# Sixteen single moves in a hand-written order of steps: polysketch attention and a multiplicative FFN on one core

## The chip, the core and the metric

The kernel runs on one core of a Trainium2 chip. The metric is the device time of one execution in microseconds (us), as the median of several runs.

## What is computed

Two blocks in a row, all in float32. The first is linear attention over 4 batches of 4 heads with 1088 tokens of 32 numbers; its feature map `phi` is the outer product of two sketches with 8 numbers each. The second is an FFN on 4352 tokens with 128 numbers, whose hidden layer (1024 wide) is the product of two projections.

```python
def phi(x):
    a = np.einsum('rd,bhsd->bhsr', S1, x)
    b = np.einsum('rd,bhsd->bhsr', S2, x)
    return np.einsum('bhsi,bhsj->bhsij', a, b).reshape(*x.shape[:-1], r * r)
q_p, k_p = (phi(q), phi(k))
kv = np.einsum('bhsf,bhsd->bhfd', k_p, v)
z = np.sum(k_p, axis=2)
num = np.einsum('bhsf,bhfd->bhsd', q_p, kv)
den = np.einsum('bhsf,bhf->bhs', q_p, z)[..., None] + 1e-06
x = (num / den)            # bridge: (B,H,S,D) -> (B*S, H*D)
h = (x @ w1) * (x @ w2) @ w3
out = h @ w_out
```

## The kernel before

**How the work is cut.** `make_steps` (L150) defines 1179 named steps, each with one or a few instructions, and the kernel issues them in the order of the hand-written list `ORDER` (L75). Each engine (PE the matrix unit, DVE the vector engine, ACT the scalar engine, POOL GpSimd, SP the engine that issues DMAs) executes its own instructions in that order, chained one behind the other; between engines only true dependences on data and buffers wait. So a move in `ORDER` changes the work of those engines alone that find other steps of theirs between the old place and the new.

**Which engine a step takes** is set by four sets of names: what calls `on(name)` goes to DVE, or to POOL where the name is in `POOL` (L53), or to ACT (`ACTS`); a copy by `cp(name)` goes to ACT, or to DVE where the name is in `CPV` (L65).

**Which buffer it takes** is dealt by `SLOTS` (L28): for each kind of tile a string with one digit per tile in the order in which the tiles are made. "b" deals the eight PSUM banks, "m" 32 SBUF buffers of 2 KB a row, "l" 13 larger ones. A tile waits for the last reader of the tile that had its buffer before.

**The stages**, by the names of their steps:

- `k0` to `k3` are the four batches of k. `k3.gram0` to `k3.gram4` (L659) build a Gram matrix with 144 small matmuls 32x64 and 32x32, `Gm`, `Gt`, `Ga`, `Gb`, `Gc` split it (on DVE, `Gc` on ACT), and `T0`, `T1`, `N0`, `N1` are small products behind it. `k2.rest0`, which the Gram of k2 needs, and `k2.kT1`, `k3.rest0` prepare k on POOL and ACT.
- `q0` to `q3` are groups of 512 tokens of q, `q4` and `q6` groups of 1024, `qr` the last 256. A group goes through `max`, `l1`, `l2`, `rm` (peak and scales), `sl`, `sca`, `sh` (splits), `al`, `bs` (the two sketches), `p01`, `p2`, `p12`, `dn`, `de`, `rc` (denominator), `phi0` (L1509, outer product), `pT0` (L1517, a transposition on DVE), `x` (L1527, 64 products 32x32 into four banks) and `xT0` to `xT3` (L1540, copies out of the banks: four on DVE or ACT for each step of a wide group). `q4.ns` (L1494) is a row of short POOL operations for scales.
- `w0` to `w10` turn the weights from 64-bit words into float32: `load`, `c` (ACT), `m`, `j` (DVE, some `m` on ACT), `a0`, `a1` (POOL). At most four large loads are under way (`UNDER_WAY`, L1880). `f0` to `f7` fold `w3` and `w_out` into `w3o`. `s.RC` (three copies on POOL) and `s.AR` spread the sketch matrices.
- FFN groups `g0` to `g3` have 512 tokens each. For each of eight column blocks c: `g{n}.{c}a` (L1799, product with w1), `g{n}.{c}c` (L1804, copy to SBUF), `g{n}.{c}b` (L1809, product with w2), `g{n}.{c}m` (L1815, their product on DVE, called ab). `g{n}.{c}o` (L1835) multiplies ab with `w3o` and sums up in one bank of the group, `g{n}.oT` (L1842) transposes that bank on DVE, and the store follows. The last 256 tokens are the group `gr`.
- FFN groups 4 to 7 go two by two by a scheme with seven products for eight (`seven`, L1633; names `h4`, `h6`). For each of four blocks i and each of the two weights (`a`, `b`): products `h4.2a1` to `h4.2a7` (L1673; an `a` and a `b` product use half of PE's rows each), copies and sums `c` to `i` (L1680 and others), multiplications `m11`, `m12`, `m22` (L1707), `m21`, sums `T1` to `T4` (L1727 to L1742), and products `P1` to `P7` (L1759; 64 columns each, low or high half).

**Around the change.** Ahead of `q3.x` DVE takes the multiplications of groups 1 and 2, `k3.Gm` to `k3.Gb`, `k3.kT0` and the copy `g2.3c`; `q3.x` takes four banks, the last of which DVE's multiplications give back. Ahead of `qr.x` the products `g1.7o`, `g0.1o`, `g0.0o`, `g0.5o`, `g0.7o`, `g1.0o`, `g3.5o` stand on PE, then `q6.x`; on DVE `g0.oT` and then `qr`'s chain from `p01` to `phi0`, with `p01`, `p2`, `p12`, `bs` on POOL, and behind it the eight copies of `q6.xT0` and `q6.xT2` and `qr.pT0`; `q6.xT1` and `q6.xT3` are ACT's. `h4.s2` and the `T` sums of `POOL` are POOL's.

Of the kernel before, what the change touches and what calls it, by code (L numbers as in the profile page):

```python
# [86 lines left out]
q1.Ct g0.4c g0.4b q1.sh q1.sl k1.rest0 g0.7b w0.c1 g0.7a k1.abt w0.j1 k1.gram0 w0.c0 q1.scy k1.gram1 kh2.load q1.sca  # L87
q2.tr g0.5c q1.al q1.p01 q1.p2 k1.gram2 k1.gram3 kr1.abc k1.gram4 w6.load w0.m0 g0.6b w0.j0 g0.7c g0.7m k1.Gm q1.p12
k1.Gc g0.0a w2.load w0.a1 q1.dn q1.de q1.rc q1.bs k1.Gt g0.3a k1.Ga k2.kT1 k1.Gb g0.3c q1.restT g0.2a q1.phi k1.T0
k1.T1 q1.pt0 g0.4m w0.a0 q2.max q2.l2 g0.6a k1.Ta k2.lead0 k2.rest0 g0.1a g0.2c k1.Tc g0.5b q3.tr g0.5m k1.Tb q1.pc0  # L90
q1.pt1 g0.1b w9.load s.RC k1.N0 s.AR q2.l1 q2.rm v3.zero q1.pc1 k1.N1 q1.x g0.6c g0.1c k1.Na k1.Nr k3.zero k2.gram0
# [1843 lines left out]
```

## Time and profile before

| | us |
|---|---|
| median of 3 runs | 246.07 |
| lowest and highest run | 245.98, 246.84 |
| the profiled execution's own time | 246.81 |
| its span, from first to last instruction | 245.0 |
| PE busy, share of the span | 237.3, 97% |
| DVE busy | 208.7, 85% |
| POOL busy | 162.5, 66% |
| ACT busy | 123.6, 50% |

The profile lists busy time by engine, the chain of work that ended last (followed back from the last instruction), and for PE what each idle stretch waited for (a row "PE tile line <- releaser tile line: total, count, longest"). A row of the grouped instructions in a window reads: start in us, busy time, engine, line, operation, out<-in, size, count; a bracket at its end is the idle time of the engine just before and what ended it. A row of the table by stretches reads: window, its length, then busy time and count of PE, PE's weight loads, DVE, ACT and POOL, then the granted PE clock, the DMA share and GB/s. A row of the chain reads: start, length, engine, tile, line. A float32 product of 512 columns leaves two records on PE, so `x10` there are five products.

### The profile page before, as it was taken

The page shows a single profiled execution, that of the slowest core. Times are in us where ns is not written, and L with a number is a line of the kernel's source. Part 1 is how long each engine was busy: PE and PEld are TensorE (multiplying, and loading weights), DVE is VectorE, ACT ScalarE, POOL GpSimd, SP SyncE. Part 2 cuts the span into 40 slices and gives each one's busy share as a digit, 9 for nine tenths or more (in the row PEclk, how much of TensorE's full clock was granted, in tenths as well). Part 3 has the DMA queues.
Part 4 walks back from the last instruction along what each step waited for, and adds up shares of the span by engine and source line. Part 5 has one row for each costly group of instructions (what it writes and reads, how often), then busy time and mean ns, then how long its engine had stood idle before and what let it go on. Part 6 is the DMA issues. An engine that isn't in the chain of part 4 may idle for free.

```text
span 245.0 us, 6748 instructions
## 1 busy us (share of the span) xinstructions
PE 237.3 (97%) x2724; PEld 132.8 (54%) x2724; DVE 208.7 (85%) x421; ACT 123.6 (50%) x245; POOL 162.5 (66%) x204
## 2 busy tenths in 40 slices
...
GB/s 209 258 112 321 147 226 218 46 208 209 238 117 262 191 207 206 37 1 3 3 0 3 1 0 3 59 112 3 1 0 0 0 3 0 0 1 3 11 92 91
DMA packets 31935, 22.06 MB, mean 90 GB/s; under 512 B 21280, under 2 KB 26528, under 8 KB 31904
## 3 DMA queue, kind: packets, MB, share of 16 engines
...
q14 instruction: 10, 0.08, 0.1%
...
## 4 chain that ended last, share of the span: by engine, by line
PE 84%; DVE 8%; ACT 3%; issue 2%; POOL 1%; ACTq 0%; POOLq 0%; DVEq 0%
PE ps_X L1673 11%; PE a_ps L1799 10%; PE ps_o L1759 10%; PE b_ps L1809 10%; PE ps_o L1835 9%; PE ps_Y L1673 6%; PE ps_w3o L534 5%; PE idle_ps L255 4%; PE ps_Z L1673 3%; PE ps_ac L1374 2%; PE ps_x L1527 2%; PE ps_g L659 2%; PE ps_kv L769 2%; PE ps_or L1824 2%; DVE ab L1815 2%
## 5 line engine op out<-in xcount | busy, mean ns | idle before, releaser
L1673 PE MATMUL ps_X<-xd,wv 64*128 64x512 f32 x112 | 36.3, 593 | 0.0
L1799 PE MATMUL a_ps<-xT,w 128*128 128x512 f32 (+1 forms) x80 | 35.9, 560 | 0.0
L1809 PE MATMUL b_ps<-xT,w 128*128 128x512 f32 (+1 forms) x80 | 35.6, 555 | 0.0
L1804 ACT COPY ffa<-a_ps 128x512 f32<-128x512 f32 (+1 forms) x37 | 19.8, 541 | 28.7 <-PE a_ps L1799 25.6
L1707 POOL TENSOR_TENSOR hc<-hc 128x512 f32<-128x512 f32 x16 | 20.6, 1302 | 13.8 <-DVE hc L1685 13.5
L1835 PE MATMUL ps_o<-ab,w3o 128*128 128x512 f32 x64 | 29.6, 600 | 0.0
L1680 ACT COPY hc<-ps_X 128x512 f32<-128x512 f32 x38 | 21.1, 591 | 16.4 <-PE ps_X L1673 13.5
L1815 DVE TENSOR_TENSOR ab<-ffa,b_ps 128x512 f32<-128x512 f32 (+1 forms) x40 | 24.0, 624 | 5.1 <-PE b_ps L1809 4.2
L501 POOL TENSOR_TENSOR w3c<-w3c,cv_m 128x512 int32<-128x512 int32 x16 | 21.2, 1344 | 4.4 <-DVE w3c L495 4.4
L1799 PEld LDWEIGHTS a_ps<-xT,w 128*128 128x128 f32 x80 | 14.1, 189 | 14.4 <-issue 8.6
L1673 PEld LDWEIGHTS ps_X<-xd,wv 64*128 64x128 f32 x112 | 15.4, 186 | 12.0 <-issue 9.2
L1809 PEld LDWEIGHTS b_ps<-xT,w 128*128 128x128 f32 x80 | 14.4, 190 | 13.1 <-issue 8.3
L1673 PE MATMUL ps_Y<-xd,wv 64*128 64x512 f32 x48 | 19.6, 594 | 0.0
L1835 PEld LDWEIGHTS ps_o<-ab,w3o 128*128 128x128 f32 x64 | 11.6, 190 | 13.4 <-issue 13.0
L534 PEld LDWEIGHTS ps_w3o<-wo,w3T 128*128 128x128 f32 x128 | 15.3, 192 | 2.4 <-issue 2.4
L534 PE MATMUL ps_w3o<-wo,w3T 128*128 128x128 f32 x128 | 15.7, 276 | 0.0
L1759 PE MATMUL ps_o<-hc,w3o 128*64 128x512 f32 x32 | 15.1, 595 | 0.0
L1759 PE MATMUL ps_o<-tt,ws 128*64 128x512 f32 x32 | 13.7, 595 | 0.0
L263 ACT ACTIVATE cv_c<-raw 128x1024 f32<-128x1024 f32 (+1 forms) x13 | 13.0, 1017 | 0.0
L1680 ACT COPY hc<-ps_Y 128x512 f32<-128x512 f32 x14 | 8.1, 593 | 9.7 <-PE ps_Y L1673 7.0
L1540 ACT COPY xd<-ps_x 64x256 f32<-64x256 f32 x24 | 8.8, 367 | 7.2 <-PE ps_o L1835 6.8
L538 ACT COPY w3o<-ps_w3o 128x128 f32<-128x128 f32 x8 | 2.1, 272 | 19.7 <-PE ps_w3o L534 19.7
...
## 6 DMA issues: line engine op xcount, KB each, us to landing
...
```

What stands on the lines that cost most here:

```text
L263: act.activation(dst, hi.bitcast(F32), ACT.Prelu, scale=2.0 ** -112, alpha=-2.0 ** 32)
L501: pool.tensor_tensor(d, d, x["m"][:, i * 512:(i + 1) * 512], ALU.add)
L534: pe.matmul(t["o"], w3T[ko][:, c], wo[:, c], start=c == 0, stop=c == NC - 1)
L1673: pe.matmul(x[bank], stat(j, u)[:, i * 128:(i + 1) * 128], rows(j, u), start=new, stop=True, tile_position=(u * 64, 0), skip_group_check=True)
L1680: cp(n(y))(x[k], x[bank])
L1707: on(f"h{g}.{i}m{k}").tensor_mul(both[0][k], both[0][k], both[1][k])
L1759: pe.matmul(acc_o[bank][half[0]:half[1]], w(i), x(i), start=n == 1, stop=n == (2 if j == 3 else 4), tile_position=(0, half[0]), skip_group ...
L1799: pe.matmul(x["a"][:, :w], w_of(0, c), xT[g][:, c0:c0 + w], start=True, stop=True)
L1804: cp(f"g{g}.{c}{su}c")(x["s"][:, :w], x["a"][:, :w])
L1809: pe.matmul(x["b"][:, :w], w_of(1, c), xT[g][:, c0:c0 + w], start=True, stop=True)
L1815: dve.tensor_mul(ab_sb[g, c][:, c0:c0 + w], x["s"][:, :w], x["b"][:, :w])
L1835: pe.matmul(o_ps[g], w3o[:, c], ab_sb[g, c], start=n == 1, stop=n == NC)
```

## The change

The first 182 steps of `ORDER` stay as they are; SP's order stays as a whole. Behind them steps move, two change engine, and `SLOTS` follows (three strings, a few digits each):

- `s.RC` goes from behind `w9.load` up to behind `w0.c0`: on POOL ahead of `q1.sca`.
- `k1.T0` goes ahead of `k2.kT1`: on PE ahead of `g0.2a`.
- `g2.6c` and `k3.rest0` go behind `g2.4b`: on ACT `w5.m` now stands ahead of `g2.6c`.
- `q2.restT`, `w6.m`, `w5.j`, `w2.j` go ahead of `q4.l2`: on ACT `w6.m` now stands ahead of it.
- `g2.1a` goes from behind `w5.m` to behind `k3.Gc`: on PE behind the Gram of k3 and `g2.2a`.
- `g2.3c` goes from DVE to ACT.
- `g2.5m` goes ahead of `g2.7c` and `g2.7m`; `qr.l1`, `qr.rm` ahead of `q4.sl`; `qr.sl` ahead of `q6.dn`.
- `g1.7o` goes from behind `q6.phi1` to behind `g0.oT`: on PE behind `g3.5o`, still ahead of `q6.x`.
- `qr.pT0` goes right behind `qr.phi0`: on DVE ahead of the eight copies.
- `h4.2ac`, `h4.2a6` go ahead of `h4.1ah`: on PE `h4.2a6` ahead of `h4.2a2`, `h4.2b6`.
- `h4.2T2` goes from POOL to DVE.
- `h6.1P4`, `h6.0P1`, `h6.3m21` go ahead of `h6.3m22`.

With the banks dealt anew, `q3.x` waits for `g2.3m` and no longer for `g2.1m`, `qr.x` waits for the copies of `q6.xT2` too, `g1.0b` now waits for `g2.6c`, and `q4.l1` no longer waits for `f2.t`.

```diff
 POOL = set("""
-    g4.oS g5.oS g6.oS g7.oS h4.0T1 h4.0T2 h4.0T3 h4.0m12 h4.0m22 h4.1T2 h4.1m11 h4.1m12 h4.2T2
-    h4.2m11 h4.2m12 h4.2m22 h4.3m11 h4.s2 h4.s4 h6.0T2 h6.0m11 h6.0m12 h6.0m22 h6.1T2 h6.1T3 h6.1m11
+    g4.oS g5.oS g6.oS g7.oS h4.0T1 h4.0T2 h4.0T3 h4.0m12 h4.0m22 h4.1T2 h4.1m11 h4.1m12 h4.2m11
+    h4.2m12 h4.2m22 h4.3m11 h4.s2 h4.s4 h6.0T2 h6.0m11 h6.0m12 h6.0m22 h6.1T2 h6.1T3 h6.1m11 h6.1m12
...
 CPV = set("""
-    g0.0c g0.1c g2.3c h4.1ac h4.1ad h6.1bc h6.2ad k0.kT1 k1.kvc k2.kT1 k2.kq k3.kT0 k3.kT1 k3.kq
-    q0.xc0 q0.xc1 q6.xT0 q6.xT2
+    g0.0c g0.1c h4.1ac h4.1ad h6.1bc h6.2ad k0.kT1 k1.kvc k2.kT1 k2.kq k3.kT0 k3.kT1 k3.kq q0.xc0
+    q0.xc1 q6.xT0 q6.xT2
...
-k2.Na g1.3m g2.6c k3.rest0 g2.4a g2.3a w5.m g2.1a g2.4b g1.0b k2.Nr q3.rc g1.1m g1.4m g1.6b k2.Nb g0.2b kr1.kp w6.j
-q4.tr g2.4c g1.6m w7.load w7.c q3.bs q4.max q4.l2 w3.load w9.a0 k3.gram0 q2.restT w6.m w5.j w2.j k3.gram1 k3.gram2
-q3.load w7.j q3.phi0 k3.gram3 k3.gram4 g2.2a k3.Gc g1.0m w2.a0 g2.6b g2.0a g2.4m g2.1c f6.t w6.a0 w4.load g2.3b w2.a1
+k2.Na g1.3m g2.4a g2.3a w5.m g2.4b g2.6c k3.rest0 g1.0b k2.Nr q3.rc g1.1m g1.4m g1.6b k2.Nb g0.2b kr1.kp w6.j q4.tr
+g2.4c g1.6m w7.load w7.c q3.bs q4.max q2.restT w6.m w5.j w2.j q4.l2 w3.load w9.a0 k3.gram0 k3.gram1 k3.gram2 q3.load
+w7.j q3.phi0 k3.gram3 k3.gram4 g2.2a k3.Gc g2.1a g1.0m w2.a0 g2.6b g2.0a g2.4m g2.1c f6.t w6.a0 w4.load g2.3b w2.a1
...
-g1.5o q4.xT0 qr.sl qr.sc qr.al q6.rc q6.bs q4.xT1 q6.nb q6.na q6.nm q6.nr q6.ne v.1 q6.nn q6.phi0 q4.xT3 q6.phi1 g1.7o
-o.S3 q6.pT0 h4.s1 q6.pT1 g0.1o g0.0o g0.5o g0.7o g1.0o h4.s2 g3.5o g0.oT q6.x g1.1o g2.5o qr.p01 qr.p2 qr.p12 qr.dn
-g3.3o qr.de qr.rc qr.bs qr.phi0 g3.2o q6.xT0 q6.xT1 q6.xT2 o.S1 g2.2o v.2 g3.7o q6.xT3 qr.pT0 qr.x qr.xT0 g1.3o g2.0o
+de g1.5o q4.xT0 qr.sc qr.al q6.rc q6.bs q4.xT1 q6.nb q6.na q6.nm q6.nr q6.ne v.1 q6.nn q6.phi0 q4.xT3 q6.phi1 o.S3
+q6.pT0 h4.s1 q6.pT1 g0.1o g0.0o g0.5o g0.7o g1.0o h4.s2 g3.5o g0.oT g1.7o q6.x g1.1o g2.5o qr.p01 qr.p2 qr.p12 qr.dn
+g3.3o qr.de qr.rc qr.bs qr.phi0 qr.pT0 g3.2o q6.xT0 q6.xT1 q6.xT2 o.S1 g2.2o v.2 g3.7o q6.xT3 qr.x qr.xT0 g1.3o g2.0o
```

**First place: DVE ahead of `q3.x`.** The rows are the end of DVE's work ahead of that step: `G_t` is `k3.Gt`, `kT` is `k3.kT0`, the copy `ffa` is `g2.3c`, `G_a` and `G_b` are `k3.Ga` and `k3.Gb`.

```order
 L201 SCALAR_TENSOR_TENSOR G_t<-G_g,ps_g 128x32
 L720 STREAM_TRANSPOSE kT<-kh 128x512
-L1804 COPY ffa<-a_ps 128x512
 L204 SCALAR_TENSOR_TENSOR G_a<-G_g,G_t 128x32
 L865 TENSOR_TENSOR G_b<-ps_g,G_a 128x32
```

The copy has left DVE; ACT takes it among its copies of group 2. On PE the place where `g2.1a` arrives is the end of the Gram of k3; `ps_g` is the Gram's bank, `w_81` the converted weights.

```order
 L659 MATMUL ps_g<-kk 32x64
 L659 MATMUL ps_g<-k,kk 32x32
-L1799 MATMUL a_ps<-xT,w_81 128x512
+L1799 MATMUL a_ps<-xT,w_81 128x512 x2
 L1809 MATMUL b_ps<-xT,w_81 128x512
 L1799 MATMUL a_ps<-xT,w_81 128x512
```

Two a products follow the Gram now, `g2.2a` and `g2.1a`, in place of one.

**Second place: PE ahead of `q6.x`.** The rows are the eight o products there before the change; `ps_o_2228` is the bank of group 1, `ps_o_2214` that of group 0, and `ab_1251` is the ab of `g1.7o`.

```order
L1835 MATMUL ps_o_2228<-ab_1349,w3o_83 128x512
L1835 MATMUL ps_o_2228<-ab_1251,w3o_83 128x512
L1835 MATMUL ps_o_2214<-ab_976,w3o_83 128x512
L1835 MATMUL ps_o_2214<-ab_1309,w3o_83 128x512
L1835 MATMUL ps_o_2214<-ab_900,w3o_83 128x512
L1835 MATMUL ps_o_2214<-ab_824,w3o_83 128x512
L1835 MATMUL ps_o_2228<-ab_1597,w3o_83 128x512
L1835 MATMUL ps_o_2137<-ab_2254,w3o_83 128x512
```

After the change the same eight stand so (two ab tiles carry other numbers since copies are made in another order):

```order
L1835 MATMUL ps_o_2228<-ab_1349,w3o_83 128x512
L1835 MATMUL ps_o_2214<-ab_976,w3o_83 128x512
L1835 MATMUL ps_o_2214<-ab_1309,w3o_83 128x512
L1835 MATMUL ps_o_2214<-ab_903,w3o_83 128x512
L1835 MATMUL ps_o_2214<-ab_827,w3o_83 128x512
L1835 MATMUL ps_o_2228<-ab_1597,w3o_83 128x512
L1835 MATMUL ps_o_2137<-ab_2254,w3o_83 128x512
L1835 MATMUL ps_o_2228<-ab_1251,w3o_83 128x512
```

`g1.7o` has gone from the second place to the last, and the four products that fill group 0's bank stand one place earlier. `g0.oT` waits for the last of them.

**Third place: DVE behind `qr.phi0`.** `s_rc` is `qr.rc`, `ph` is `qr.phi0`, `pT` is `qr.pT0`, the eight `xd` are `q6.xT0` and `q6.xT2`.

```order
 L1454 RECIPROCAL s_rc<-s_rc 128x8
 L1509 TENSOR_TENSOR ph<-s_al,s_bs 128x512
+L1517 STREAM_TRANSPOSE pT<-ph 128x512
 L1540 COPY xd<-ps_x 64x256 x8
-L1517 STREAM_TRANSPOSE pT<-ph 128x512
 L1842 STREAM_TRANSPOSE oT<-ps_o 128x512 x3
 L1654 TENSOR_TENSOR xd<-xd 128x512
```

The transposition that `qr.x` needs now stands ahead of the eight copies and no longer behind them.

More of the change, by code (lines that the diff above doesn't have):

```diff
@@ L29 @@
     "b":
-        "012345670214657210671306537457462512346127340273014526045421752342140327540542370673245716"
-        "210605643174306534710724534104562761504514502371054643535436051532410354273245554744570504"
+        "012345670214657210671306537457462512346127340273014526045721472352140327540542370673245716"
+        "210605643174306437107523543106572361507514502371054643535436051532410354273245554744570504"
         "7734023146507073701426351241254057163771361764573436046273673572571236574127105",
@@ L34 @@
     "l":
-        "0123456789a7486797c0864b7705995a34b20138c73b92bc0b4879c146a281ba56271a564b60303643a19ca32c"
+        "0123456789a7486797c0864b7705995a34210b38c73b92bc0b4879c146a281ba56271a564b60303643a19ca32c"
         "c2076b",
     "m":
-        "0123456789aejo96p3ke3rfjo7p5t8g50lfin6q8o4donmgp19fh2og3hi5601au6v4jm8emhubcusv6vjgo2olsjs"
+        "0123456789aejo96p3ke3rfjo7p5t8g50lfin6q8o4donmgp19fh2og3hi5601au6v4jm8emhubcusv62jgo6olsjs"
         "aolp8s0h8roj26gk1ivl8hb3mcu0a5pn7tfd9qe0umb4p5j1e2tkmgjeno5rcub7tjkume92fka4ud5tkbigpq10lv"
@@ L53 @@
 POOL = set("""
-    g4.oS g5.oS g6.oS g7.oS h4.0T1 h4.0T2 h4.0T3 h4.0m12 h4.0m22 h4.1T2 h4.1m11 h4.1m12 h4.2T2
-    h4.2m11 h4.2m12 h4.2m22 h4.3m11 h4.s2 h4.s4 h6.0T2 h6.0m11 h6.0m12 h6.0m22 h6.1T2 h6.1T3 h6.1m11
-    h6.1m12 h6.1m22 h6.2T1 h6.2T4 h6.2m11 h6.3T3 h6.3m11 h6.s1 h6.s2 h6.s4 k0.Nf k0.Nh k0.Nr k0.kp1
-    k1.Nr k1.kp1 k2.kp0 k2.kp1 k2.rest0 k3.kp0 k3.kp1 q0.al q0.p01 q0.phi1 q0.sca q1.al q1.bs q1.p12
+    g4.oS g5.oS g6.oS g7.oS h4.0T1 h4.0T2 h4.0T3 h4.0m12 h4.0m22 h4.1T2 h4.1m11 h4.1m12 h4.2m11
+    h4.2m12 h4.2m22 h4.3m11 h4.s2 h4.s4 h6.0T2 h6.0m11 h6.0m12 h6.0m22 h6.1T2 h6.1T3 h6.1m11 h6.1m12
+    h6.1m22 h6.2T1 h6.2T4 h6.2m11 h6.3T3 h6.3m11 h6.s1 h6.s2 h6.s4 k0.Nf k0.Nh k0.Nr k0.kp1 k1.Nr
+    k1.kp1 k2.kp0 k2.kp1 k2.rest0 k3.kp0 k3.kp1 q0.al q0.p01 q0.phi1 q0.sca q1.al q1.bs q1.p12
     q1.phi q1.sca q2.bs q2.p2 q2.phi0 q2.sc q2.sl q3.al q3.bs q3.p01 q3.p12 q3.p2 q3.phi0 q3.sc
@@ L86 @@
 w0.load k1.lead0 q0.xc0 q0.xc1 k0.kq w1.a1 k2.max q0.xt1 k1.ab q0.xT0 q0.xT1 g0.4a q1.load g0.5a q1.sm w0.m1 q1.st
[L87 to L91, printed above, removed]
+q1.Ct g0.4c g0.4b q1.sh q1.sl k1.rest0 g0.7b w0.c1 g0.7a k1.abt w0.j1 k1.gram0 w0.c0 s.RC q1.scy k1.gram1 kh2.load
+q1.sca q2.tr g0.5c q1.al q1.p01 q1.p2 k1.gram2 k1.gram3 kr1.abc k1.gram4 w6.load w0.m0 g0.6b w0.j0 g0.7c g0.7m k1.Gm
+q1.p12 k1.Gc g0.0a w2.load w0.a1 q1.dn q1.de q1.rc q1.bs k1.Gt g0.3a k1.Ga k1.T0 k2.kT1 k1.Gb g0.3c q1.restT g0.2a
+q1.phi k1.T1 q1.pt0 g0.4m w0.a0 q2.max q2.l2 g0.6a k1.Ta k2.lead0 k2.rest0 g0.1a g0.2c k1.Tc g0.5b q3.tr g0.5m k1.Tb
+q1.pc0 q1.pt1 g0.1b w9.load k1.N0 s.AR q2.l1 q2.rm v3.zero q1.pc1 k1.N1 q1.x g0.6c g0.1c k1.Na k1.Nr k3.zero k2.gram0
 g0.1m k2.gram1 k2.gram2 q3.max k2.gram3 g0.0c k2.kT0 k1.Nb q1.xT k2.gram4 q3.l2 k2.ab q2.A0 q2.C0 q2.C1 q3.l1 k1.kp0
@@ L107 @@
 q4.st k2.kv0 w4.a1 k3.kp0 k2.kv3 k2.kv1 k2.kv2 k2.kvr q4.sh qr.l2 k3.kv0 k3.kv1 f3.t k2.kvc k3.kv3 k3.kv2 k3.Na w4.a0
-q4.sl q4.sc qr.l1 qr.rm q4.al k3.kvr k3.kvc g3.4a q6.l2 g3.4c g3.4b q4.p01 k3.Nr g3.3b q6.l1 w8.c g3.5a k3.Nb g2.4o
+qr.l1 qr.rm q4.sl q4.sc q4.al k3.kvr k3.kvc g3.4a q6.l2 g3.4c g3.4b q4.p01 k3.Nr g3.3b q6.l1 w8.c g3.5a k3.Nb g2.4o
 g3.4m f1.t f3.m w10.c k3.kqt g3.5c w8.m g3.3m q4.p2 q6.rm k3.kq f1.m f1.o q6.A0 q6.C0 w10.j q6.C1 g3.1o f3.o w8.j
```

11 lines of the change are left out of this document (6 added, 5 removed).

## The prediction, made before the changed kernel ran

> **What bounds the kernel now.** I read the page first, then who waited for whom on PE, then the busy time by stretch.
>
> ```profile
> PE 237.3 (97%) x2724; PEld 132.8 (54%) x2724; DVE 208.7 (85%) x421; ACT 123.6 (50%) x245; POOL 162.5 (66%) x204
> ...
> PE 84%; DVE 8%; ACT 3%; issue 2%; POOL 1%; ACTq 0%; POOLq 0%; DVEq 0%
> ...
> PE ps_g L659 <- issue: 1.6, 2, 1.1
> ...
> PE ps_ph L1246 <- POOL ph L1208: 0.6, 1, 0.6
> PE ps_x L1527 <- DVE pT L1517: 0.4, 1, 0.4
> ...
> 74.00:85.00 11.00, 10.89 (x213) 6.62 (x212) 10.65 (x20) 7.43 (x9) 8.58 (x7) 1.00 0.91 226
> 85.00:152.00 67.00, 67.00 (x795) 38.85 (x786) 60.19 (x117) 31.23 (x65) 48.64 (x41) 1.00 0.19 45
> ```
>
> The reader is to see an engine without room: PE is busy 97% of the span and is 84% of the chain that ended last; from 85 to 152 us it is busy 67.00 of 67.00. The work on PE is the same before and after, so the change can gain only what PE now idles and can lose only where it makes PE idle. DVE, at 85%, gates PE at a few places; a step that leaves DVE or comes earlier there counts only if such a place is behind it. So I went from one PE wait to the next and asked which moves reach it.
>
> **The wait of q3.x at 84 us** (moves of g2.1a, g2.3c). The same 64 products for q2 stand at 65 us. In order: two PE rows of q2.x, the row of q3.x, three pieces of the chain, then rows of DVE, PE (two) and ACT.
>
> ```profile
> 64.97 0.96 PE L1527 MATMUL ps_x<-pT,kq 32*32 32x128 f32 x57
> ...
> 65.74 0.30 PE L1527 MATMUL ps_x<-pT,kq 32*32 32x128 f32 x3
> ...
> 84.02 1.57 PE L1527 MATMUL ps_x<-pT,kq 32*32 32x128 f32 x64
> ...
> 81.83 0.58 DVE ffa L1804
> ...
> 83.29 1.20 DVE ab L1815 x2
> 84.49 0.04 issue
> 84.53 1.05 PE ps_x L1527 x54
> ...
> 74.32 0.69 DVE L1815 TENSOR_TENSOR ab<-ffa,b_ps 128x512 f32<-128x512 f32 x1 [1.63 <-PE b_ps L1809]
> ...
> 67.25 4.45 PE L1799 MATMUL a_ps<-xT,w 128*128 128x512 f32 x10
> 71.54 3.60 PE L1809 MATMUL b_ps<-xT,w 128*128 128x512 f32 x8
> ...
> 79.77 0.59 ACT L1804 COPY ffa<-a_ps 128x512 f32<-128x512 f32 x1 [0.96 <-PE a_ps L1799]
> ```
>
> q2.x lasts from 64.97 to 66.04, 1.07 us; q3.x starts at 84.02, stands still until DVE's ab at 84.49 has given a bank back, and lasts 1.57. The wait costs 0.50. DVE had waited 1.63 us for a b product until 74.32 and was then busy without a break. Two things shorten that run. Moving g2.1a behind the k3 Gram takes one product out from ahead of g1.6b: from row to row five a products (two records each) take 71.54 - 67.25 = 4.29, so 0.86 each, and DVE starts 0.86 earlier. The copy g2.3c (0.58 in the chain) leaves DVE. And because the copies are dealt other banks, q3.x now waits for g2.3m, no longer for g2.1m behind it (half of 1.20). So the DVE run reaches the needed point at 84.49 - 0.86 - 0.58 - 0.60 = 82.45, 1.57 ahead of PE's 84.02: the wait goes, **-0.50**. PE does g2.1a's 0.86 later, behind g2.2a, so from there its order costs the same. g2.3c costs ACT 0.59, in a stretch where ACT idles 0.96 before one copy alone and is busy 7.43 of 11.00. What is late next at 84.02 is PE itself. The products that come 0.86 earlier (g2.4b to g2.2a) read xT and banks that have long been free; g1.0b now waits for g2.6c, which stands behind w5.m on ACT; two ACT copies and one w5.m between 68.3 and 70.7 leave it there 0.9 us early.
>
> **The wait of qr.x at 152.6 us** (moves of g1.7o, qr.pT0). Rows of PE (four), DVE (four), ACT and POOL:
>
> ```profile
> 136.83 8.75 PE L1835 MATMUL ps_o<-ab,w3o 128*128 128x512 f32 x20
> 145.51 1.50 PE L1527 MATMUL ps_x<-pT,kq 32*32 32x256 f32 x64
> ...
> 150.04 2.31 PE L1835 MATMUL ps_o<-ab,w3o 128*128 128x512 f32 x5
> 152.75 0.84 PE L1527 MATMUL ps_x<-pT,kq 32*32 32x64 f32 x64 [0.40 <-DVE pT L1517]
> ...
> 144.76 0.72 DVE L1842 STREAM_TRANSPOSE oT<-ps_o 128x512 f32<-128x512 f32 x1 [0.93 <-PE ps_o L1835]
> ...
> 147.28 1.20 DVE L1509 TENSOR_TENSOR ph<-s_al,s_bs 128x512 f32<-128x512 f32 x1 [0.41 <-POOL s_bs L1459]
> 148.40 3.46 DVE L1540 COPY xd<-ps_x 64x256 f32<-64x256 f32 x8
> 151.89 0.71 DVE L1517 STREAM_TRANSPOSE pT<-ph 128x512 f32<-128x512 f32 x1
> ...
> 148.10 3.12 ACT L1540 COPY xd<-ps_x 64x256 f32<-64x256 f32 x8 [6.78 <-PE ps_o L1835]
> ...
> 143.94 1.26 POOL L1649 TENSOR_TENSOR xd<-xd 128x512 f32<-128x512 f32 x1 [0.68 <-PE ps_o L1835]
> ```
>
> Unhindered, such a product starts 0.07 before the modelled end of the one ahead (145.51 against 136.83 + 8.75 = 145.58); qr.x starts 0.40 after it, so the wait costs **0.47**. Turning pT0 and the copies round alone would gain nothing: qr.x needs the transposition and, for its banks, the last of DVE's eight copies, and the sum of both is the same. What makes room is g1.7o. It goes from ahead of six products to behind them, so g0.oT, for which DVE idles 0.93, can come 0.86 earlier; POOL's link beside it (idle 0.68) only 0.68. With 0.68, phi0 ends at 147.80, pT0 at 148.51, behind both q6.x (147.01) and the product that frees xd (148.10), and the copies end at 151.97. PE would be free for qr.x at 152.28: 0.31 ahead, the wait goes. If the 0.50 above comes through, both sides come earlier alike. Behind it no PE wait shows until the end, and DVE and POOL there start from PE's products.
>
> **h4.2T2 from POOL to DVE.** Rows of DVE (two), POOL (two), PE:
>
> ```profile
> 183.56 1.77 DVE L1707 TENSOR_TENSOR hc<-hc 128x512 f32<-128x512 f32 x1
> ...
> 185.86 0.68 DVE L1742 TENSOR_TENSOR tt<-tt,hc 128x512 f32<-128x512 f32 x1
> ...
> 183.19 1.59 POOL L1732 TENSOR_TENSOR tt<-hc,tt 128x512 f32<-128x512 f32 x1 [1.21 <-DVE tt L1727]
> 184.75 0.65 POOL L1494 TENSOR_TENSOR nz<-nz 128x8 f32<-128x8 f32 x1
> ...
> 186.66 0.59 PE L1759 MATMUL ps_o<-hc,w3o 128*64 128x512 f32 x1
> ```
>
> DVE gets 0.68 more just ahead of h4.3m22, T3 and h4.0T4, whose result (186.54) h4.0P4 takes at 186.66: 0.12 of room. But the multiplication beside POOL's T2 took 1.77, from 183.56 to 0.55 behind POOL's end at 184.78, where its like takes 0.68. With T2 gone from POOL it should take 0.68: +0.68 - 1.09 = -0.41 on DVE, so PE keeps its room. I take 0; the bounds are 0 and, if the 1.77 stays, 0.68 - 0.12 = +0.56. [...]
>
> **The rest, at nothing.** Rows of PE and POOL:
>
> ```profile
> 38.00 0.66 PE L1246 MATMUL ps_ph<-ident,ph 128*128 128x128 f32 x4 [0.55 <-POOL ph L1208]
> ...
> 29.04 1.50 POOL L1161 TENSOR_TENSOR s_hl<-s_hl,ay_C 128x128 f32<-128x128 f32 x1 [0.95 <-DVE s_hl L1157]
> ...
> 42.66 0.96 POOL L378 COPY RC<-Sc 128x32 f32<-128x32 f32 x3
> ```
>
> s.RC, 0.96, now fills POOL's 0.95 of idle time ahead of 29.04: at most 0.01 late, and k2.rest0, which k2.gram0 needs, ends ahead of it either way. k1.T0 between two a products may cost PE a switch, hidden in the 0.55 for which q1.pt0 waits for POOL; without that cover 0.1 to 0.2. w6.m ahead of q4.l2 puts q4.l2 1.2 later on ACT, but q4.l1 waits for other work until 86. SP's and POOL's orders there don't change. g2.5m ahead of g2.7c, qr.rm, qr.sl, h4.2ac/h4.2a6 (PE's a/b pairs stay pairs) and h6.1P4 lie beside a PE that is busy throughout; bounds 0 to +0.3 together, taken as 0.
>
> **The sum**: -0.50 - 0.47 = -0.97. The profiled execution took 246.81 us (span 245.0 and 1.81 around it) and would take 245.84. It was 0.74 above the median of 246.07; from the median the sum gives **245.1**.
>
> **Rivals.**
> - One of the two waits stays: qr.x's, if the small chain between oT and phi0 on POOL and DVE doesn't follow. For it: 0.31 of room on five hand-overs. 246.07 - 0.50 = 245.6.
> - T2 delays DVE: -0.97 + 0.56, so 245.7.
> - The gains don't reach the end: PE comes earlier and meets DVE at the next narrow place (DVE 60.19 of 67.00 in the long stretch), 246.1.
> [...]
>
> **How the numbers follow.** Forecast 0.50; one wait stays 0.17; T2 0.10; nothing reaches the end 0.08; dry Gram 0.07; more than forecast (0.3 to 0.6 from DVE's lead at places that I hold for free) 0.08. The range runs from 244.5 (forecast and that extra) to 246.4 (dry Gram). 0.5%, about what a measurement of this kernel can tell, is 1.23 us: below 244.84 lie the extra case and the lower edge of the forecast, 0.24; above 247.30 hardly any case but a dry Gram with T2's loss, 0.06; the rest, 0.70, is within.
>
> **What would show it.** Right: q3.x lasts about 1.1 us with no bank wait; no idle time ahead of qr.x, pT ahead of the eight copies; the multiplication behind T2 takes 0.7; both Grams as before. Wrong: an idle row of PE at the k3 Gram, at g1.0b, or in the P products near 186, or a span that doesn't shrink although both waits are gone.

## The result, and the profile after

| | before | after |
|---|---|---|
| median of 22 runs each, us | 246.28 | 245.39 |
| lowest to highest | 245.82 to 248.05 | 244.41 to 246.77 |
| ratio after to before | | 0.9958, 95% interval 0.9944 to 0.9971 |
| span of the profiled execution | 245.0 | 244.1 |

The changed kernel is faster by 0.42%, about 1.0 us. These lines of its page and of its busy time by stretch answer to those of the prediction:

```profile
PE 236.2 (97%) x2724; PEld 129.8 (53%) x2724; DVE 206.7 (85%) x421; ACT 123.5 (51%) x246; POOL 161.9 (66%) x203
...
PE 87%; DMA 5%; ACT 2%; POOL 2%; DVE 1%; issue 1%; POOLq 0%; SPq 0%
...
74.00:85.00 11.00, 11.00 (x224) 6.82 (x228) 10.96 (x19) 7.74 (x12) 9.07 (x8) 1.00 0.93 217
85.00:152.00 67.00, 67.00 (x789) 38.76 (x780) 59.67 (x116) 31.09 (x65) 49.07 (x42) 1.00 0.19 45
152.00:240.00 88.00, 88.00 (x468) 40.98 (x468) 76.42 (x123) 33.39 (x66) 60.51 (x72) 1.00 0.13 22
```

DVE's share of the chain has gone from 8% to 1%, and from 74 to 240 us PE is busy in every stretch: 166.00 of 166.00. The list of PE's waits still names the Gram of k2, `q1.phi` and some that lie ahead of 27 us, and of the two waits of the prediction none:

```profile
PE ps_g L659 <- issue: 1.6, 2, 1.2
...
PE ps_ph L1246 <- POOL ph L1208: 0.2, 1, 0.2
```

**At q3.x.** Rows of PE (two), DVE (three) and POOL of the changed kernel, from its list by time:

```profile
84.39 1.07 PE L1527 MATMUL ps_x<-pT,kq 32*32 32x128 f32 x64
85.39 0.25 PE L883 MATMUL ps_T<-RS,G_a 128*32 128x32 f32 x2
...
81.27 1.30 DVE L204 SCALAR_TENSOR_TENSOR G_a<-G_g,G_t 128x32 f32<-128x32 f32 x1
82.60 0.19 DVE L865 TENSOR_TENSOR G_b<-ps_g,G_a 128x32 f32<-128x32 f32 x1
82.71 1.87 DVE L1815 TENSOR_TENSOR ab<-ffa,b_ps 128x512 f32<-128x512 f32 x3
...
81.25 1.28 POOL L501 TENSOR_TENSOR w3c<-w3c,cv_m 128x512 int32<-128x512 int32 x1
```

`q3.x` lasts 1.07 in place of 1.57: the 0.50 has come. But `k3.Ga` takes 1.30 (before 0.73), and it ends at 82.57 (81.27 + 1.30), 0.04 behind the POOL addition that began 0.02 ahead of it (81.25 + 1.28 = 82.53).

**At qr.x.** Rows of PE (two) and DVE (four):

```profile
146.81 5.42 PE L1835 MATMUL ps_o<-ab,w3o 128*128 128x512 f32 x12
152.15 0.85 PE L1527 MATMUL ps_x<-pT,kq 32*32 32x64 f32 x64
...
143.77 0.72 DVE L1842 STREAM_TRANSPOSE oT<-ps_o 128x512 f32<-128x512 f32 x1 [0.31 <-PE ps_o L1835]
...
146.29 1.20 DVE L1509 TENSOR_TENSOR ph<-s_al,s_bs 128x512 f32<-128x512 f32 x1 [0.41 <-POOL s_bs L1459]
147.52 0.71 DVE L1517 STREAM_TRANSPOSE pT<-ph 128x512 f32<-128x512 f32 x1
148.16 3.43 DVE L1540 COPY xd<-ps_x 64x256 f32<-64x256 f32 x8
```

`qr.x` starts at 152.15, 0.08 ahead of the modelled end of the products (146.81 + 5.42 = 152.23): no wait. The copies end at 151.59, 0.56 ahead.

**A clock that leaves the start out.** The first 47 us are the same code in all kernels but for a few moves, and yet they end at another time in every run: in after PE stands still for 0.91 at 20 us with nothing to wait for, in e12_fill for 0.63, in before not at all. So for each trace three stretches of PE are taken: from the first product of `k2.ab` (behind the Gram of k2) to that of `k3.T0` (behind `q3.x`), from there to that of `g1.3o` (behind `qr.x`), and from there to the end of PE's last product (modelled). All are read from the lists by time:

| kernel | k2.ab starts | to k3.T0 | to g1.3o | to PE's end | sum |
|---|---|---|---|---|---|
| before | 47.09 | 38.43 | 68.01 | 87.74 | 194.18 |
| after | 47.46 | 37.93 | 67.55 | 87.62 | 193.10 |
| e1_qr_both | 46.31 | 38.44 | 67.55 | 87.73 | 193.72 |
| e2_g17o | 46.38 | 38.43 | 67.73 | 87.72 | 193.88 |
| e3_pT0 | 46.28 | 38.43 | 67.88 | 87.73 | 194.04 |
| e4_banks | 46.30 | 38.06 | 68.00 | 87.74 | 193.80 |
| e5_g23c | 45.98 | 38.43 | 68.01 | 87.74 | 194.18 |
| e6_g21a | 46.14 | 37.93 | 68.00 | 87.74 | 193.67 |
| e7_T2 | 48.12 | 38.43 | 68.02 | 87.67 | 194.12 |
| e8_fetch | 46.55 | 37.93 | 67.55 | 87.62 | 193.10 |
| e9_late | 46.58 | 37.93 | 67.55 | 87.62 | 193.10 |
| e10_three | 46.39 | 37.92 | 67.56 | 87.73 | 193.21 |
| e11_Ga | 46.20 | 37.93 | 68.37 | 87.73 | 194.03 |
| e12_fill | 47.05 | 37.94 | 67.55 | 87.63 | 193.12 |

Where a stretch isn't touched it repeats within 0.02 (the first: 38.43 or 38.44 in six traces), while its start moves by 2.1 us (45.98 to 48.12). So 0.1 us can be told here, and not from medians of whole runs. From before to after the stretches shrink by 0.50, 0.46 and 0.12: 1.08 in all.

### The profile page after: what moved, and what is told of

Its sections match the earlier page's. It is cut to its first block, busy times and chain, and to the rows that moved or that the text cites. A ratio compares the mean times of both kernels' runs of the same rounds, so it can differ in the third digit from the quotient of the medians.

```text
span 244.1 us, 6745 instructions
## 1 busy us (share of the span) xinstructions
PE 236.2 (97%) x2724; PEld 129.8 (53%) x2724; DVE 206.7 (85%) x421; ACT 123.5 (51%) x246; POOL 161.9 (66%) x203
## 4 chain that ended last, share of the span: by engine, by line
PE 87%; DMA 5%; ACT 2%; POOL 2%; DVE 1%; issue 1%; POOLq 0%; SPq 0%
PE b_ps L1809 12%; PE ps_o L1835 12%; PE ps_X L1673 11%; PE a_ps L1799 11%; PE ps_o L1759 10%; PE ps_w3o L534 6%; PE ps_Y L1673 6%; PE ps_Z L1673 3%; PE ps_g L659 2%; PE ps_x L1527 2%; PE ps_ac L1374 2%; DMA qh<-in_q_dram 2%; DMA k<-in_k_dram 2%; PE ps_or L1824 2%; POOL ph L1208 1%; PE idle_ps L255 1%
## 5 line engine op out<-in xcount | busy, mean ns | idle before, releaser
L1673 PEld LDWEIGHTS ps_X<-xd,wv 64*128 64x128 f32 x112 | 14.9, 186 | 13.1 <-issue 10.9
L1497 POOL COPY nz<-nz 32x8 f32<-32x8 f32 x32 | 11.1, 347 | 1.4
```

The costliest lines, as they stand in the source:

```text
L1673: pe.matmul(x[bank], stat(j, u)[:, i * 128:(i + 1) * 128], rows(j, u), start=new, stop=True, tile_position=(u * 64, 0), skip_group_check=True)
```

## The experiments

The theory is that of the prediction: two PE waits of 0.50 and 0.47 go, and nothing else counts. The main rivals: other moves carry part of the gain, or DVE's time behind those waits is set by something that the sum had not seen. Four kernels (e4_banks, e5_g23c, e6_g21a, e11_Ga) ran once each, for the trace alone; the others ran 10 or 12 times.

### qr.x: both moves, and each alone

Label e1_qr_both: two moves in the order of before.

```diff
-g1.5o q4.xT0 qr.sl qr.sc qr.al q6.rc q6.bs q4.xT1 q6.nb q6.na q6.nm q6.nr q6.ne v.1 q6.nn q6.phi0 q4.xT3 q6.phi1 g1.7o
-o.S3 q6.pT0 h4.s1 q6.pT1 g0.1o g0.0o g0.5o g0.7o g1.0o h4.s2 g3.5o g0.oT q6.x g1.1o g2.5o qr.p01 qr.p2 qr.p12 qr.dn
-g3.3o qr.de qr.rc qr.bs qr.phi0 g3.2o q6.xT0 q6.xT1 q6.xT2 o.S1 g2.2o v.2 g3.7o q6.xT3 qr.pT0 qr.x qr.xT0 g1.3o g2.0o
+g1.5o q4.xT0 qr.sl qr.sc qr.al q6.rc q6.bs q4.xT1 q6.nb q6.na q6.nm q6.nr q6.ne v.1 q6.nn q6.phi0 q4.xT3 q6.phi1
+o.S3 q6.pT0 h4.s1 q6.pT1 g0.1o g0.0o g0.5o g0.7o g1.0o h4.s2 g3.5o g0.oT g1.7o q6.x g1.1o g2.5o qr.p01 qr.p2 qr.p12 qr.dn
+g3.3o qr.de qr.rc qr.bs qr.phi0 qr.pT0 g3.2o q6.xT0 q6.xT1 q6.xT2 o.S1 g2.2o v.2 g3.7o q6.xT3 qr.x qr.xT0 g1.3o g2.0o
```

> The kernel before with g1.7o and qr.pT0 moved, nothing else. Theory (the wait of qr.x is worth 0.47 us and nothing behind it takes it back): no idle time ahead of qr.x, time 0.47 below the kernel before, ratio 0.998. Rival (gains don't reach the end): no idle time ahead of qr.x, ratio 1.000.

Label e2_g17o has the first of the two moves (`g1.7o` behind `g0.oT`), label e3_pT0 the second (`qr.pT0` behind `qr.phi0`).

> The kernel before with g1.7o alone moved behind g0.oT; qr.pT0 stays behind the eight copies. Theory (g1.7o makes all the room): DVE's chain from oT to pT0 comes 0.68 to 0.86 earlier, pT0 ends about 0.7 to 0.8 before it did, 0.2 to 0.4 ahead of the time at which PE comes to qr.x; no idle time ahead of qr.x, ratio 0.998. Rival (the transposition ahead of the copies is what counts): the wait stays, ratio 1.000.

> The kernel before with qr.pT0 alone moved ahead of the eight copies. Theory (a sum of the same DVE work is turned round): qr.x waits as before, now for the last copy of q6.xT2 in place of pT0, about 0.40 idle, ratio 1.000. Rival (the transposition is the bottleneck): no idle time ahead of qr.x, ratio 0.998.

Ratios to before: 0.9998 (0.9974 to 1.0022), 0.9997 (0.9976 to 1.0019), 1.0000 (0.9977 to 1.0023). An interval of 0.2% to each side cannot tell 0.998 from 1.000; the times decide nothing here, the traces do. With both moves the stretch shrinks by 0.46, the whole wait. With `g1.7o` alone, PE (two rows) and DVE (two):

```profile
148.92 2.74 PE L1835 MATMUL ps_o<-ab,w3o 128*128 128x512 f32 x6
151.76 0.84 PE L1527 MATMUL ps_x<-pT,kq 32*32 32x64 f32 x64
...
147.40 3.47 DVE L1540 COPY xd<-ps_x 64x256 f32<-64x256 f32 x8 [0.36 <-PE ps_o L1835]
150.90 0.71 DVE L1517 STREAM_TRANSPOSE pT<-ph 128x512 f32<-128x512 f32 x1
```

`qr.x` starts 0.10 behind the modelled end of the products, where 0.07 to 0.08 ahead of it is usual: 0.17 to 0.18 of the wait is left, and the stretch says the same (67.73 against 67.55). The reason is in the third row: DVE comes to the copies early and then idles 0.36 for the product that frees `xd`. With `qr.pT0` alone, PE and DVE:

```profile
151.48 1.18 PE L1527 MATMUL ps_x<-pT,kq 32*32 32x64 f32 x64
...
148.35 3.43 DVE L1540 COPY xd<-ps_x 64x256 f32<-64x256 f32 x8
```

`qr.x` now starts without a wait, does the products whose banks are free, and stands still inside itself until the last copy (151.78); it lasts 1.18 in place of 0.85, and 0.13 of the 0.46 is gained. So `g1.7o` brings 0.28, `qr.pT0` alone 0.13, and both 0.46: the transposition also fills the 0.36 for which DVE would idle.

### q3.x: the three things that shorten DVE's run, each alone

Label e4_banks: no step moved; in the string of the banks `q3.x` takes bank 7 for 4, `g2.0b` 4 for 7, `g2.7b` 7 for 4.

```diff
-        "210605643174306534710724534104562761504514502371054643535436051532410354273245554744570504"
+        "210605643174306534710724534107562461507514502371054643535436051532410354273245554744570504"
```

> The kernel before with three PSUM banks dealt anew and no step moved: q3.x takes bank 7 for bank 4, so it waits for g2.3m and no longer for g2.1m behind it. Theory (each of the three shortenings ahead of q3.x alone is nearly enough): g2.3m ends 0.14 ahead of the start of q3.x (83.88 against 84.02 in the trace of before), q3.x lasts about 1.07 in place of 1.57. Rival (DVE's run comes late as a whole, the bank only names the last of it): q3.x still stands still, 1.3 or more.

Label e5_g23c: one name leaves the set of DVE's copies.

```diff
-    g0.0c g0.1c g2.3c h4.1ac h4.1ad h6.1bc h6.2ad k0.kT1 k1.kvc k2.kT1 k2.kq k3.kT0 k3.kT1 k3.kq
+    g0.0c g0.1c h4.1ac h4.1ad h6.1bc h6.2ad k0.kT1 k1.kvc k2.kT1 k2.kq k3.kT0 k3.kT1 k3.kq
```

> The kernel before with the copy g2.3c alone taken from DVE to ACT. Theory of the prediction: DVE is 0.58 earlier at g2.1m, q3.x lasts about 1.1. Rival (contention, from the trace of the changed kernel, where k3.Ga took 1.30 in place of 0.73 and ended 0.05 behind POOL's w5.a1): k3.Ga starts 0.58 earlier, beside POOL's w5.a1, waits for its end and ends where it did; q3.x lasts 1.57 as before.

Label e6_g21a: one step moved, the banks of before dealt in the new order of tiles.

```diff
-k2.Na g1.3m g2.6c k3.rest0 g2.4a g2.3a w5.m g2.1a g2.4b g1.0b k2.Nr q3.rc g1.1m g1.4m g1.6b k2.Nb g0.2b kr1.kp w6.j
+k2.Na g1.3m g2.6c k3.rest0 g2.4a g2.3a w5.m g2.4b g1.0b k2.Nr q3.rc g1.1m g1.4m g1.6b k2.Nb g0.2b kr1.kp w6.j
...
-q3.load w7.j q3.phi0 k3.gram3 k3.gram4 g2.2a k3.Gc g1.0m w2.a0 g2.6b g2.0a g2.4m g2.1c f6.t w6.a0 w4.load g2.3b w2.a1
+q3.load w7.j q3.phi0 k3.gram3 k3.gram4 g2.2a k3.Gc g2.1a g1.0m w2.a0 g2.6b g2.0a g2.4m g2.1c f6.t w6.a0 w4.load g2.3b w2.a1
```

> The kernel before with g2.1a alone moved behind the Gram of k3. Theory: DVE's run comes 0.86 earlier as far as g2.1m, which then ends 0.36 ahead of the start of q3.x (83.63 against 84.02); q3.x lasts 1.07. Rival (contention eats part of it): POOL's additions hold k3.Ga, g2.1m ends later than 84.02 in the time of the trace of before and q3.x lasts 1.2 to 1.5.

`q3.x` with other banks, and with `g2.1a` moved (here DVE's row of three multiplications too):

```profile
83.24 1.07 PE L1527 MATMUL ps_x<-pT,kq 32*32 32x128 f32 x64
84.36 0.25 PE L883 MATMUL ps_T<-RS,G_a 128*32 128x32 f32 x2
```

```profile
83.07 1.07 PE L1527 MATMUL ps_x<-pT,kq 32*32 32x128 f32 x64
...
81.40 1.88 DVE L1815 TENSOR_TENSOR ab<-ffa,b_ps 128x512 f32<-128x512 f32 x3
```

Both take the stall out of `q3.x`. The banks alone gain 0.37, since `k3.T0` behind it, whose bank the third multiplication `g2.6m` gives back, starts 0.05 behind the end of `q3.x` (83.24 + 1.07 = 84.31) in place of 0.07 ahead of it. `g2.1a` alone gains 0.50, all there is; the second multiplication ends 0.4 ahead of `q3.x`. The copy `g2.3c` gains nothing (38.43); PE, DVE and POOL there:

```profile
82.92 1.56 PE L1527 MATMUL ps_x<-pT,kq 32*32 32x128 f32 x64
...
80.65 1.30 DVE L204 SCALAR_TENSOR_TENSOR G_a<-G_g,G_t 128x32 f32<-128x32 f32 x1
...
80.65 1.26 POOL L501 TENSOR_TENSOR w3c<-w3c,cv_m 128x512 int32<-128x512 int32 x1
```

`k3.Ga` starts where the copy would have stood, beside POOL's `w5.a1`, and ends at 81.95, 0.04 behind it. The group of such operations in the trace of after (shortest, median and longest in ns) says how long the other three take, with no POOL addition running when they begin: 0.19.

```profile
L204 DVE SCALAR_TENSOR_TENSOR G_a<-G_g,G_t x4: 192/193/1301, 15.4 to 81.3; 128x32 f32<-128x32 f32 x4
```

So in before, too, most of its 0.73 was waiting. It ran from 82.33 to 83.06, beside a POOL addition that ends at 83.01; the rows of both:

```profile
82.33 0.73 DVE L204 SCALAR_TENSOR_TENSOR G_a<-G_g,G_t 128x32 f32<-128x32 f32 x1
...
81.72 1.29 POOL L501 TENSOR_TENSOR w3c<-w3c,cv_m 128x512 int32<-128x512 int32 x1
```

The copy had stood in that wait and cost nothing. Beside the same additions the multiplications into `ab`, one input of which is a bank, are not held: three take 1.87 (83.20 in before), and one takes 0.67 (80.41), where one with POOL idle took 0.69 (74.32). `k3.Ga` has two inputs in SBUF; whether that makes the difference no run shows.

Label e11_Ga takes e5_g23c and turns two steps round, to put `k3.Ga` beside another addition.

```diff
-g2.2b g2.2c g2.0c w6.a1 g2.1b q3.pT0 k3.Gm g0.2m k3.Gt k3.kT0 v3.load w7.m f6.m w5.a1 w5.a0 g2.3c k3.Ga k3.Gb g2.3m
+g2.2b g2.2c g2.0c w6.a1 g2.1b q3.pT0 k3.Gm g0.2m k3.Gt k3.Ga k3.kT0 v3.load w7.m f6.m w5.a1 w5.a0 g2.3c k3.Gb g2.3m
```

> The kernel before with g2.3c on ACT, as in the run that moved it alone, and k3.Ga turned round with the transposition k3.kT0 ahead of it on DVE. Theory (k3.Ga reads two SBUF operands and cannot end before the POOL addition beside it ends): k3.Ga now stands beside w6.a1 and ends 0.05 behind that, 1.2 earlier than behind w5.a1; the 0.58 of the copy comes through and q3.x lasts 1.07. Rival (k3.Ga is slow for another reason, or the copy's 0.58 is lost elsewhere): k3.Ga takes 0.7 or more without touching the end of w6.a1, and q3.x lasts about 1.5 as it did with g2.3c alone.

PE (three rows), DVE (three) and POOL (two):

```profile
83.13 1.07 PE L1527 MATMUL ps_x<-pT,kq 32*32 32x128 f32 x64
...
90.67 1.02 PE L1799 MATMUL a_ps<-xT,w 128*128 128x512 f32 x2
91.72 0.70 PE L1799 MATMUL a_ps<-xT,w 128*128 128x512 f32 x1
...
80.33 0.60 DVE L204 SCALAR_TENSOR_TENSOR G_a<-G_g,G_t 128x32 f32<-128x32 f32 x1
...
84.57 1.82 DVE L495 TENSOR_SCALAR w3c<-cv_c 128x1024 int32<-128x1024 int32 x1
...
90.98 0.69 DVE L1815 TENSOR_TENSOR ab<-ffa,b_ps 128x512 f32<-128x512 f32 x1
...
79.61 1.27 POOL L501 TENSOR_TENSOR w3c<-w3c,cv_m 128x512 int32<-128x512 int32 x1
...
82.09 3.75 POOL L501 TENSOR_TENSOR w3c<-w3c,cv_m 128x512 int32<-128x512 int32 x3
```

`k3.Ga` ends at 80.93, 0.05 behind the end of `w6.a1` (80.88), and the 0.50 at `q3.x` comes through. That the POOL addition holds it is thereby shown: with the copy on ACT as in e5_g23c and another addition beside it, its end follows that addition. In all fourteen traces it ends 0.04 to 0.06 behind one.

But the next stretch is 0.36 longer (68.37), all of it ahead of 93 us. Part of it stands in the rows: `g3.6a`, whose bank `g2.7m` gives back, starts 1.05 behind `g3.3a` in place of 0.86, just behind that multiplication (90.98 + 0.69 = 91.67). DVE is late there because of `w3.j`, the row of L495: 1.82, where before it took 1.12. It ends at 86.39, 0.55 behind POOL's last of three additions (85.84), and these had not moved. In before it ended 0.55 behind the same addition too (87.27 and 86.72), in e6_g21a 0.56 (85.47 and 84.91), but in e6_g21a POOL's additions come 0.86 earlier with the rest. So DVE's lead was taken back at the next place where POOL holds it, and the rival "the gains don't reach the end" is real here. e4_banks, with DVE no earlier at that place, loses nothing (68.00): in its dealing `g3.6a` takes a bank that `g2.7b` doesn't have.

### h4.2T2 alone on DVE

Label e7_T2:

```diff
-    g4.oS g5.oS g6.oS g7.oS h4.0T1 h4.0T2 h4.0T3 h4.0m12 h4.0m22 h4.1T2 h4.1m11 h4.1m12 h4.2T2
+    g4.oS g5.oS g6.oS g7.oS h4.0T1 h4.0T2 h4.0T3 h4.0m12 h4.0m22 h4.1T2 h4.1m11 h4.1m12
```

> The kernel before with h4.2T2 alone on DVE. Theory: T2 takes DVE 0.68, the multiplication h4.3m22 behind it shrinks from 1.77 to 0.68, PE stays busy throughout, ratio 1.000. Rival (m22 keeps its 1.77, beside another POOL instruction): DVE is 0.68 late at h4.0T4, PE waits about 0.56 at h4.0P4, ratio 1.002.

DVE's rows of T2 and of the multiplication behind it:

```profile
184.60 0.68 DVE L1732 TENSOR_TENSOR tt<-hc,tt 128x512 f32<-128x512 f32 x1
185.20 0.68 DVE L1707 TENSOR_TENSOR hc<-hc 128x512 f32<-128x512 f32 x1
```

The multiplication has gone from 1.77 to 0.68, so DVE does one instruction more and is done sooner. The ratio is 1.0006 (0.9983 to 1.0029), the third stretch 87.67 for 87.74. A row of PE in before says where the 0.07 was:

```profile
188.39 0.64 PE L1759 MATMUL ps_o<-tt,ws 128*64 128x512 f32 x1
```

This is `h4.3P5`, which reads DVE's `h4.3T1`. That ends at 188.34, 0.05 ahead of it; the row takes 0.64 where its like takes 0.59, and from there on its half of the columns runs 0.07 behind the other (188.87 and 188.80). In e7_T2 `h4.3T1` ends 0.53 ahead of the same product, which takes 0.59. So it is in every trace: 0.64 in the nine with T2 on POOL, 0.59 in the five with T2 on DVE.

### Three of the sixteen moves

Label e10_three: before with `g2.1a`, `g1.7o` and `qr.pT0` moved, as in e6_g21a and e1_qr_both together.

> The kernel before with three of the sixteen moves: g2.1a, g1.7o, qr.pT0, and nothing else (engines as before). Theory (these three carry the whole gain, the rest is worth nothing): q3.x lasts 1.07, no idle time ahead of qr.x, behind 50 us PE's times shift by 0.97 against the trace of before, ratio 0.996 like the changed kernel. Rival (other moves carry a part): a shift clearly below 0.97 behind 50 us.

```profile
83.32 1.07 PE L1527 MATMUL ps_x<-pT,kq 32*32 32x128 f32 x64
...
151.08 0.85 PE L1527 MATMUL ps_x<-pT,kq 32*32 32x64 f32 x64
```

Ratio 0.9958 (0.9937 to 0.9980), the changed kernel's own. The stretches shrink by 0.51, 0.45 and 0.01, so 0.97 of the 1.08; the other thirteen moves bring 0.11 behind 47 us, of which 0.07 is the move of T2. Between 25 and 47 us they bring nothing: from the start of the matmuls of L1287 to that of `k2.ab`, without the stall in the Gram of k2, PE needs 20.29 in before and in after (25.65 to 47.09 less 1.15; 26.01 to 47.46 less 1.16).

### What is left: the Gram of k2 and q1.pt0

PE still stands inside the Gram of k2. Label e8_fetch puts `q1.x`, four products of 512 columns, into it; label e9_late puts it one step further.

```diff
-q1.pc0 q1.pt1 g0.1b w9.load k1.N0 s.AR q2.l1 q2.rm v3.zero q1.pc1 k1.N1 q1.x g0.6c g0.1c k1.Na k1.Nr k3.zero k2.gram0
-g0.1m k2.gram1 k2.gram2 q3.max k2.gram3 g0.0c k2.kT0 k1.Nb q1.xT k2.gram4 q3.l2 k2.ab q2.A0 q2.C0 q2.C1 q3.l1 k1.kp0
+q1.pc0 q1.pt1 g0.1b w9.load k1.N0 s.AR q2.l1 q2.rm v3.zero q1.pc1 k1.N1 g0.6c g0.1c k1.Na k1.Nr k3.zero k2.gram0
+g0.1m k2.gram1 q1.x k2.gram2 q3.max k2.gram3 g0.0c k2.kT0 k1.Nb q1.xT k2.gram4 q3.l2 k2.ab q2.A0 q2.C0 q2.C1 q3.l1 k1.kp0
```

> The changed kernel with q1.x (four products of 512 columns, 1.08 us) moved from ahead of the Gram of k2 to between its second and third step. Theory (instruction supply: the stall of 1.15 to 1.6 inside the Gram is the time by which 144 small products use up the instructions that are there; a wide product among them gives the next ones time to come): the idle time inside the Gram shrinks by up to 1.08, and the time by about that much, ratio to the kernel before about 0.992. Rival (the next instructions come at a fixed time whatever stands ahead of them): the stall ends when it did, PE has only done the same work in another order, and the ratio stays that of the changed kernel, 0.996.

> The changed kernel with q1.x moved one step further than in the run before, behind the third step of the Gram of k2, right ahead of the step in which PE stood still. Theory left over (the stall ends a fixed time behind the instruction packet that is fetched when the Gram begins): PE does 1.08 of work in that time and the stall of 1.1 to 1.2 shrinks below 0.3; ratio to the kernel before about 0.992. Rival (the stall follows a number of instructions and not the clock): the stall stays 1.1, ratio 0.995 to 0.996.

The row behind the stall, in before, after, e8_fetch and e9_late:

```profile
46.62 0.22 PE L659 MATMUL ps_g<-k,kk 128*32 128x32 f32 x1 [1.15 <-issue]
```

```profile
46.98 0.19 PE L659 MATMUL ps_g<-k,kk 128*32 128x32 f32 x1 [1.16 <-issue]
```

```profile
46.07 0.19 PE L659 MATMUL ps_g<-k,kk 128*32 128x32 f32 x1 [1.06 <-issue]
```

```profile
46.11 0.19 PE L659 MATMUL ps_g<-k,kk 128*32 128x32 f32 x1 [0.87 <-issue]
```

With 1.08 of work put ahead of it the stall is 0.10 and 0.29 shorter than in after, but with the old order it varies as much from kernel to kernel (1.44 in e1_qr_both, 0.89 in e10_three). And nothing was gained: from the matmuls of L1287 to `k2.ab`, without the stall, PE needs 20.62 and 20.60 here in place of 20.29. Ratios 0.9948 (0.9930 to 0.9967) and 0.9959 (0.9926 to 0.9991), that of the changed kernel within their intervals. My theory of the supply of instructions, in the form that a wide product buys the time, has fallen; that the stall follows a number of instructions fits but isn't shown. One packet of the instruction queue moves at 44.27 in after, 0.07 behind the first matmul of the Gram (44.20), and the next at 48.18, 1.20 behind the stall's end (46.98): none lands where it ends. What ends it stays open.

Label e12_fill moves a product ahead of `q1.pt0`, for which PE waits 0.24 in after.

```diff
-q1.phi k1.T1 q1.pt0 g0.4m w0.a0 q2.max q2.l2 g0.6a k1.Ta k2.lead0 k2.rest0 g0.1a g0.2c k1.Tc g0.5b q3.tr g0.5m k1.Tb
+q1.phi k1.T1 g0.4m g0.6a q1.pt0 w0.a0 q2.max q2.l2 k1.Ta k2.lead0 k2.rest0 g0.1a g0.2c k1.Tc g0.5b q3.tr g0.5m k1.Tb
```

> The changed kernel with one product, g0.6a (0.86), moved ahead of q1.pt0, for which PE waits 0.24 at 38.4 us for POOL's q1.phi. Theory (a wait in front of which free work stands is worth its own length, and what comes 0.6 later has room: q1.pc0 waits 0.39 on ACT, q1.pt1 feeds a copy that waits 1.29): no idle time ahead of q1.pt0, PE 0.24 earlier from there on, ratio to the kernel before about 0.995. Rival (the chain q1.pt0, q1.pc0, q1.pt1, q1.pc1 sets the start of q1.x): q1.x waits for q1.pc1 by 0.3 or more, and the ratio stays 0.996.

PE in after, and with the product moved:

```profile
37.75 0.25 PE L889 MATMUL ps_T<-RS,G_a 128*32 128x32 f32 x2
...
38.37 0.66 PE L1246 MATMUL ps_ph<-ident,ph 128*128 128x128 f32 x4 [0.24 <-POOL ph L1208]
38.86 1.88 PE L1799 MATMUL a_ps<-xT,w 128*128 128x512 f32 x4
40.58 1.02 PE L1809 MATMUL b_ps<-xT,w 128*128 128x512 f32 x2
```

```profile
37.35 0.25 PE L889 MATMUL ps_T<-RS,G_a 128*32 128x32 f32 x2
...
37.65 1.12 PE L1799 MATMUL a_ps<-xT,w 128*128 128x512 f32 x2
38.62 0.60 PE L1246 MATMUL ps_ph<-ident,ph 128*128 128x128 f32 x4
39.18 1.12 PE L1799 MATMUL a_ps<-xT,w 128*128 128x512 f32 x2
40.14 1.02 PE L1809 MATMUL b_ps<-xT,w 128*128 128x512 f32 x2
```

The wait is gone, and yet from `k1.T1` to `g0.5b` PE needs 2.79 in place of 2.83; behind that no wait shows ahead of `q1.x`, so the rival of the chain is not what took the gain. Two products in a row behind `q1.pt0` took 1.72 from start to start of the next (38.86 to 40.58), 0.86 each; torn apart, each directly behind small ones, they take 0.97 (37.65 to 38.62) and 0.96 (39.18 to 40.14): 0.21 of the 0.24. Why the first of the two, which in after stands behind `q1.pt0` too, took 0.86 there is not shown. Ratio 0.9952 (0.9932 to 0.9972): not told apart from the changed kernel, and no version that beats it.

## Why the prediction was right

The forecast was 245.1 from a median of 246.07, a gain of 0.97; measured are 245.39 from 246.28, 0.89 between the medians and 1.03 by the ratio, and 1.08 behind 47 us in the traces.

- **The wait of q3.x, -0.50**: measured 0.50. Of the three shortenings that the sum added up, `g2.1a` alone carries it. The banks alone would have brought 0.37. The 0.58 of `g2.3c` failed as a step: it was swallowed by POOL's hold on `k3.Ga`. In after `g2.3m`, which `q3.x` needs, ends at about 83.39 (the row of three begins at 82.71, and one alone takes 0.68), 1.00 ahead of `q3.x` and not 1.57: what is missing is the 0.57 by which `k3.Ga` grew, from 0.73 to 1.30.
- **The wait of qr.x, -0.47**: measured 0.46. That `g1.7o` makes the room was right; that the turned order alone gains nothing was wrong by 0.13, since `qr.x` can begin while the last copies run. The room was 0.56 and not 0.31: counted from `k2.ab`, `g0.oT` comes 1.36 earlier than in before, 0.50 of it from `q3.x` and 0.86 from `g1.7o`, and `phi0` follows by the same 1.36 (100.19 and 98.83), so POOL's 0.68 was no bound. My expectation for `g1.7o` alone missed the 0.36 for which DVE waits for `xd`.
- **T2, 0**: the trade of 0.68 more against 1.09 less came as worked out, and `h4.0P4` kept its room. The sum looked at that product alone; `h4.3P5` behind it had none (0.05), and that is the 0.07.
- **The rest, 0**: within 0.05 in the third stretch (87.62 against 87.67 with T2 alone). The cover that was named for `k1.T0` held, but its price was too low: the wait for POOL's `q1.phi` shrank from 0.55 to 0.24 while PE's way to `k2.ab` stayed the same, so putting `k1.T0` between two a products cost 0.31 and not 0.1 to 0.2. Without the wait it would have been lost.
- **The dry Gram**: the range's 246.4 and the chances of a dry Gram take it that the Gram of k3 can stall as that of k2 does, 1.15 (46.62 in before), for want of instructions; no run shows that want. In the Gram of k3 PE did not stall (from 74 to 85 us it is busy 11.00 of 11.00), and the stall in the Gram of k2 stayed, at 1.16.
- **The gains reach the end**: every trace with both waits gone keeps 0.97 or more to PE's last product. e11_Ga shows that this was not certain: with POOL's additions left where they were and the banks of before, 0.36 of 0.50 was lost within 10 us.
